# Windowed attention before a feed-forward layer: the attention recast in blocks of 32 queries over 128 keys each

## The chip, the cores and the metric

One core of a Trainium2 chip runs the kernel. The metric is the device time of one execution in microseconds (us), the median over runs.

## What is computed

Eight batches, eight heads, 512 local and 32 global positions, head size 64. A local query sees the 32 global keys and the local keys at most 32 positions away; a global query sees all 544 keys. The attention output (rows of 8 x 64 = 512 values, 544 rows a batch) goes through a feed-forward layer (FFN) with 2048 hidden values.

```python
s_ll = np.where(np.abs(pos[:, None] - pos[None, :]) <= 32, scale * q_l @ k_l.T, -1e9)
a_l = sm(np.concatenate([scale * q_l @ k_g.T, s_ll], axis=-1))
out_l = a_l @ np.concatenate([v_g, v_l])
out_g = sm(scale * q_g @ k_all.T) @ v_all
h = x @ w_in
out = (h - np.tanh(h)) @ w_out
```

Everything is float32, the FFN weights come in as float64.

## The kernel before, in words

Every FFN operand is held as two tiles, the value rounded to TensorE's one-pass float32r format (`hi`) and the remainder (`lo`); a product is three one-pass matmuls, hi*hi, hi*lo and lo*hi. A chunk of the FFN is one batch's 512 local rows: 16 steps, each with 12 matmuls of 512 columns at L1520 (`add_hidden`), tanh on ScalarE, a subtraction on VectorE, the split into `g hi` and `g lo` (L1537 is the low part), and 12 matmuls of 512 columns at L1568 (`add_out`). A last, smaller chunk does the 256 global rows.

Attention goes by pairs of heads, 32 pairs in all, four to a batch. The two heads lie on partitions 0 to 63 and 64 to 127. A pair goes in four tiles of 128 queries. A tile's scores are taken over 224 keys (192 around the tile and the 32 global ones), L1149 in `scores`. For batches 2 to 7 the keys and queries are split into hi and lo (`add_split`) and each score tile is three one-pass matmuls; for batches 0 and 1 they are full float32 matmuls. The mask is added and the row's extreme taken on VectorE (L1458), the exponential on ScalarE (L1465), the reciprocal on VectorE (L1221, L1222), the scaling on GpSimd (L1228). TensorE turns the probabilities (L1170 in `transposes`, matmuls with the identity), two copies bring them to `keys_first`, and `add_product` multiplies them with the values (L1247), four key ranges for each half of the queries. `PARTS` lists the ranges; the values lie in six overlapping ranges of 96 local rows and the 32 global ones. The scores of the global queries are at L1339 (L1079 and L1080 in the first two batches), their probabilities are turned on VectorE (L1381, L1384), in the first two batches on TensorE (L1117).

The order of the work is made when the program is built. Class `Order` holds every operation with an engine (or several to choose from), an estimated duration, a due time and what it reads and writes; `run` lists them by a simulated clock. Eight PSUM banks are dealt out: banks 0 to 3 to attention and to the FFN's hidden step, banks 4 to 7 to the FFN's output. `add_visit` glues several attention operations together so that TensorE does them one right after the other; such a visit asks for all its banks at once. In `add_both` a visit is a pair's transposes of one half followed by scores of another half, which takes four banks. `fill` (L1814) puts matmuls of no use into TensorE's early gaps. Batch 0's attention comes first, with nothing beside it but the loading and splitting of weights; from then on, batch b's attention is woven into batch b-1's FFN chunk.

The first loads of a pair's keys and queries come row by row and TensorE turns them (L1046); from batch 2 on they come in blocks that VectorE turns (L1285).

Of the kernel before, what the change touches and what calls it, by code (L numbers as in the profile page):

```python
# [18 lines left out]
KC = 224  # L19
KG = 352  # L20
# [29 lines left out]
class Order:  # L50
# [14 lines left out]
    def add(self, eng, fn, due, r=(), w=(), res=(), alloc=(), free=(), lat=0.0, xfer=0.0, rows=1.0, ldw=0.107, tail=0.107, lock=False, mode="f", glue=None):  # L65
# [12 lines left out]
        for k in tuple(w) + tuple(res):  # L78
            for x in self.readers.get(k, ()):
                before[id(x)] = x  # L80
        for x in before.values():
            x.succ[id(o)] = o
            o.n += 1
# [121 lines left out]
def kernel(ctx, tc, q_l, k_l, v_l, q_g, k_g, v_g, w_in, w_out, out):  # L205
# [14 lines left out]
    NPG = 736  # L220
    pg = cp.tile([P, NPG], F32, name="pg")
    idr = cp.tile([P, P], F32R, name="idr")
    idn = f32(idr)
    first_kw2 = cp.tile([P, 2 * KG], F32, name="first_kw2", tag="kw")
    first_g = cp.tile([P, H // 2, G], F32, name="first_g", tag="kgt")
# [3 lines left out]
    raw1, kq = rawkq[:, :S], rawkq[:, S:]  # L229
# [4 lines left out]
    gq = cp.tile([P, H // 2, 2, 2, G], F32R, name="gq")  # L234


    prob2 = [t.rearrange("p (a c) -> p a c", a=2)[:, j] for t in tt_ for j in range(2)]

# [12 lines left out]
    first_raw = [first_raw[:, 0], first_raw[:, 1], rawkq.rearrange("p (a t h d) -> p a t h d", a=2, t=NT, h=2)]  # L251
    first_kw = cp.tile([P, 2, 2 * S], F32, name="first_kw", tag="x_lo1")
    first_kw = [first_kw[:, 0, :2 * KG], first_kw[:, 1, :2 * KG], first_kw2]
    first_q = cp.tile([P, 4 * DM], F32, name="first_q", tag="w_out_lo4")
    wide = [wpair, first_q[:, 2 * DM:].rearrange("p (n k) -> p n k", k=2), stage[:, 0], stage[:, 1]]
    first_q = [first_q[:, :S], first_q[:, S:2 * S], cp.tile([P, S], F32, name="first_q2", tag="hi0")]
    first_q = [x.rearrange("p (t c) -> p t c", t=NT) for x in first_q]
    keys_first = cp.tile([P, 2, 2, 2, 384], F32, name="keys_first", tag="kf")
    values = cp.tile([P, 2, 6, D], F32, name="values")

    SETS = [[f"{n}{u}" for n in ("rk", "rq", "pw", "pk", "pq")] for u in range(2)] + [["raw", "kq", "kw0", "kg0", "hk0"]]


    kw_parts = Later(cp, [P, 2 * KG], "kw"), Later(cp, [P, 2 * KG], "hl")
    q_parts = Later(cp, [P, S], "hi0"), Later(cp, [P, S], "wraw2")
    gk = Later(cp, [P, 2, H // 2, G], "kgt")
# [5 lines left out]
    masks = [cp.tile([P, KC], BF16, name=f"mask{j}") for j in range(NT)]  # L272
    stats = [cp.tile([P, 24], F32, name=f"st{j}") for j in range(2)]
    gt = cp.tile([P, 6, G], F32, name="gt")
    prob = [cp.tile([P, 2 * KC + G], F32, name=f"prob{j}") for j in range(2)]
    prob = [prob[t // 2][:, t % 2 * KC:t % 2 * KC + 256] for t in range(NT)]
    first_m = cp.tile([P, 2 * KG], F32, name="first_m", tag="hl")
# [607 lines left out]
    def base(i):  # L885
        if i < H:
            return i * P0
# [963 lines left out]
```

## Time and profile before

| | us |
|---|---|
| median of 3 runs | 975.21 (974.84 to 975.99) |
| span of the profiled execution, first to last instruction | 973.7 |
| TensorE (PE) busy in it | 960.3 |
| VectorE (DVE) busy | 580.3 |
| ScalarE (ACT) busy | 452.1 |
| GpSimd (POOL) busy | 387.3 |

The profile is one execution, and of its own time the page gives the span alone; the median of the runs is 1.5 us above it, 0.15%. Busy times of PE count a matmul from its start to its modelled end, and neighbours overlap, so the spacing of starts is the better measure of what a matmul costs. An x and a number behind a group is its count of instructions. A float32 matmul call stands in the trace as two instructions (L1247 has 16 calls a pair and 32 instructions), a float32r one as one.

### The profile page before, as it was taken

What the parts mean: (1) busy time and instruction counts of PE and PEld (TensorE: products, weight loads), DVE (VectorE), ACT (ScalarE), POOL (GpSimd) and SP (SyncE); (2) the same over time, 40 slices, a digit from 0 to 9 for tenths busy, and PEclk for the clock granted to TensorE, in tenths of its full rate; (3) what the DMA queues carried; (4) which work ended last, traced back from release to release, by engine and by line L of the source; (5) the groups of instructions that cost most, each with busy time, mean ns of one, the idle gap of its engine ahead of it and who ended that gap; (6) DMA issues with size and microseconds to landing.
All of it is one profiled execution on the core that took longest, in us unless ns stands there. A gap on an engine that the chain in (4) does not pass through costs nothing.

```text
span 973.7 us, 18494 instructions
## 1 busy us (share of the span) xinstructions
PE 960.3 (99%) x6453; PEld 784.5 (81%) x6453; DVE 580.3 (60%) x1907; ACT 452.1 (46%) x1275; POOL 387.3 (40%) x526
## 2 busy tenths in 40 slices
PE   8899999999999999999999999999999999999998
PEld 5677877888888888888888888888888888888897
DVE  6997667766657555766676567657636544422211
ACT  6966575745455434654355444534535434111111
POOL 4666756534444433434234444333332332211221
PEclk9999999999999999999999999999999999999999
DMA  8565244321223121322123122221202200100010
GB/s 233 151 178 165 84 114 114 92 38 35 50 39 82 33 39 34 88 40 34 32 38 83 23 39 39 71 50 34 50 14 69 39 17 1 44 1 1 1 44 22
DMA packets 195166, 57.32 MB, mean 59 GB/s; under 512 B 179712, under 2 KB 188416, under 8 KB 195072
## 3 DMA queue, kind: packets, MB, share of 16 engines
q1 hardware_dynamic: 193728, 55.61, 24.1%
q8 instruction: 51, 0.84, 0.4%
q10 hardware_dynamic: 1344, 0.52, 0.2%
q14 instruction: 43, 0.35, 0.1%
HBM read 47.19 MB, written 8.91 MB: 58 GB/s over the span
## 4 chain that ended last, share of the span: by engine, by line
PE 93%; DVE 2%; ACT 2%; SPq 1%; issue 1%; DMA 1%; POOL 0%; POOLq 0%; DVEq 0%; ACTq 0%
PE bank L1520 39%; PE bank L1568 38%; PE bank L1247 6%; PE bank L1149 4%; PE bank L1170 4%; PE bank L1339 1%; SPq L1030 0%; PE bank L1046 0%; DMA wraw<-in_q_g_dram 0%; ACT t L1465 0%; ACT pg L1090 0%; POOL prob L1228 0%; DVE keys_first L869 0%; ACT prob L1465 0%; ACT keys_first L869 0%
## 5 line engine op out<-in xcount | busy, mean ns | idle before, releaser
L1537 POOL TENSOR_TENSOR glo<-t,ghi 128x512 fp32r<-128x512 f32 x107 | 139.1, 1301 | 328.9 <-PE bank L1568 130.0
L1528 ACT ACTIVATE t<-bank 128x512 f32<-128x512 f32 x136 | 81.3, 598 | 302.7 <-PE bank L1520 292.3
L1531 DVE TENSOR_TENSOR t<-bank,t 128x512 f32<-128x512 f32 x136 | 93.9, 691 | 202.5 <-ACT t L1528 201.8
L1228 POOL TENSOR_SCALAR prob<-prob,st 128x224 f32<-128x224 f32 x240 | 108.0, 468 | 143.3 <-DVE st L1222 124.9
L1568 PE MATMUL bank<-w_out_hi,ghi 128*128 128x512 f32 x544 | 152.7, 394 | 0.0
L1568 PE MATMUL bank<-w_out_hi,glo 128*128 128x512 f32 x544 | 151.5, 392 | 0.0
L1568 PE MATMUL bank<-w_out_lo,ghi 128*128 128x512 f32 x544 | 151.3, 392 | 0.0
L1520 PE MATMUL bank<-x_hi,w_in_hi 128*128 128x512 f32 x512 | 140.3, 397 | 0.3 <-DVE x_hi L869 0.3
L1520 PE MATMUL bank<-x_lo,w_in_hi 128*128 128x512 f32 x512 | 137.4, 390 | 0.0
L1520 PE MATMUL bank<-x_hi,w_in_lo 128*128 128x512 f32 x512 | 136.2, 390 | 0.0
L1465 ACT ACTIVATE prob<-prob,st 128x224 f32<-128x224 f32 x240 | 113.2, 475 | 14.9 <-DVE st L1458 13.7
L1458 DVE CUSTOM_DVE_ANT_0 prob<-bank,mask 128x224 f32<-128x224 f32 x240 | 80.8, 386 | 64.7 <-PE bank L1149 57.8
L1568 PEld LDWEIGHTS bank<-w_out_lo,ghi 128*128 128x128 f32 x544 | 101.1, 188 | 22.1 <-issue 1.0
L1568 PEld LDWEIGHTS bank<-w_out_hi,glo 128*128 128x128 f32 x544 | 101.0, 188 | 21.9 <-issue 0.7
L1568 PEld LDWEIGHTS bank<-w_out_hi,ghi 128*128 128x128 f32 x544 | 100.2, 188 | 22.2 <-issue 1.4
L1520 PEld LDWEIGHTS bank<-x_hi,w_in_hi 128*128 128x128 f32 x512 | 93.7, 188 | 24.7 <-issue 3.2
L1520 PEld LDWEIGHTS bank<-x_lo,w_in_hi 128*128 128x128 f32 x512 | 95.9, 188 | 20.2
L1520 PEld LDWEIGHTS bank<-x_hi,w_in_lo 128*128 128x128 f32 x512 | 95.7, 188 | 19.7
L869 ACT COPY keys_first<-bank 128x512 f32<-128x512 f32 (+2 forms) x150 | 69.9, 516 | 89.2 <-PE bank L1170 88.3
L1247 PE MATMUL bank<-keys_first,values 128*64 128x160 f32 (+3 forms) x1024 | 68.7, 276 | 2.2 <-DVE keys_first L869 1.1
L1247 PEld LDWEIGHTS bank<-keys_first,values 96*64 96x64 f32 (+1 forms) x1024 | 56.3, 136 | 9.5 <-ACT keys_first L869 2.9
L1381 DVE STREAM_TRANSPOSE gt<-pg 32x128 f32<-32x128 f32 x192 | 53.1, 276 | 10.2 <-POOL pg L1360 4.3
(164 smaller groups left out, 1222.9 us busy)
## 6 DMA issues: line engine op xcount, KB each, us to landing
values<-in_v_l_dram SPq DMA_DIRECT2D x128, 72.0 KB, 2.2
out_dram<-wpair SPq DMA_DIRECT2D x32, 256.0 KB, 2.0
rawkq<-in_k_l_dram SPq DMA_DIRECT2D x96, 64.0 KB, 2.3
rawkq<-in_q_l_dram SPq DMA_DIRECT2D x96, 64.0 KB, 2.2
values<-in_v_g_dram SPq DMA_DIRECT2D x64, 48.0 KB, 2.0
first_q<-in_moe_w_in_dram SPq DMA_DIRECT2D x6, 512.0 KB, 4.5
stage<-in_moe_w_out_dram SPq DMA_DIRECT2D x6, 512.0 KB, 4.0
stage<-in_moe_w_in_dram SPq DMA_DIRECT2D x6, 512.0 KB, 4.0
```

The lines of the kernel that those rows point to most:

```text
L869: (nc.scalar.copy if e == "A" else nc.vector.tensor_copy)(dst, src)
L1149: nc.tensor.matmul(x[:, i, :KC], q, k, start=n == 0, stop=n == len(passes) - 1)
L1228: nc.gpsimd.tensor_scalar(x, x, st[:, c:c + 1], 1.0, op0=ALU.mult, op1=ALU.mult)
L1247: nc.tensor.matmul(box["o"][h.e:h.e + D, o0:o0 + c1 - c0], values[:k, h.two, t + t // 2 + a], keys_first[:k, h.two, pair, a, c0:c1], start ...
L1381: nc.vector.transpose(gt[r, :c], view(src, [(P, c), (1, 32)], 32 * q))
L1458: nc.vector.tensor_tensor_reduce(out=self.pt(2 * tp + i)[:, :KC], in0=getattr(self, f"s_{tp}")[:, i, :KC], in1=masks[2 * tp + i], scale=-0 ...
L1465: nc.scalar.activation(x, x, AF.Exp, bias=col[:, c0 + i:c0 + i + 1], scale=-1.0, accum_out=col[:, 8 + tp + c0 + i:9 + tp + c0 + i])
L1520: nc.tensor.matmul(self.h[s][:, j * n:(j + 1) * n], w[:, cc, f * P:(f + 1) * P], self.x()[xi][:, cc, :n], start=part == 0 and cc == 0 and ...
L1528: nc.scalar.activation(tt_[q], self.h[s], AF.Tanh)
L1531: nc.vector.tensor_sub(tt_[q], self.h.pop(s), tt_[q])
L1537: eng[e].tensor_sub(gg[q][1], tt_[q], f32(gg[q][0]))
L1568: nc.tensor.matmul(self.acc[tt], g[:, j * self.n + tt * P:j * self.n + (tt + 1) * P], low_out(f) if wi else high_out(f), start=s == 0 and ...
```

## The change

Queries go in 16 blocks of 32. Each block has its own 96 local keys (`window(b)`: its own block and the two beside it) and the 32 global keys: 128 keys in place of 224. Scores are float32 for all batches and keys and queries are no longer split; TensorE is addressed as tiles of 64 rows by 32 columns (`tile_position`), one tile for each head and each of a group's four blocks. Four blocks make 128 rows by 128 keys, so a pair's probabilities are 128 x 512 for each head and are turned with 16 transposes in place of 32. The values lie in 14 ranges of 96 local rows and the 32 global ones, one for each window, so that a product has a block's window as its stationary side. Global queries' scores are float32 too, on tiles of 64 x 32, with the keys cut in two rows of 288 that have to exchange their extreme and their sum (`swap`); their probabilities are turned on VectorE for all batches. Batch 1 is loaded as the later batches are. A pair's TensorE work comes in two visits: scores and global scores, and the last pair's products with this pair's transposes. The due times, nudges and choices of engines of the order are new, and glued operations are ordered by a dependency.

The core of the diff (tables of due times left out):

```diff
-    def keys_of(x, t):
-        c = t // 2 * KG + t % 2 * P
-        return x[:, c:c + KC]
+    def window(b):
+        return min(max(b, 1), NB - 2) - 1
...
-                for i in range(2):
-                    for n, (qi, ki) in enumerate(passes):
-                        for a, x in zip(self.heads, t_):
...
-                            nc.tensor.matmul(x[:, i, :KC], q, k, start=n == 0, stop=n == len(passes) - 1)
...
+        def scores(self):
...
+                t_ = self.box["s"] = [bank([P, S], tags[n]) for n in names]
+                for t in range(NT):
+                    for i in range(4):
+                        b = 4 * t + i
+                        for c, o, n in ((W * window(b), 0, 3 * W), (S, 3 * W, G)):
+                            for h, x in enumerate(t_):
+                                r = slice(64 * h, 64 * h + 64)
+                                nc.tensor.matmul(x[W * i:W * i + W, t * P + o:t * P + o + n], q[r, W * b:W * b + W], kw[r, c:c + n],
+                                                 start=True, stop=True, tile_position=(64 * h, W * i), skip_group_check=True)
...
+        def global_scores(self):
...
+                for i in range(3):
+                    for h, x in enumerate(t_):
+                        r, o = slice(64 * h, 64 * h + 64), 64 * h
+                        c = 3 * W * (2 - i)
+                        nc.tensor.matmul(x[o:o + W, 3 * W * i:3 * W * i + 3 * W], q[r, 1, self.jj], kw[r, c:c + 3 * W],
+                                         start=True, stop=True, tile_position=(o, o), skip_group_check=True)
+                        if i == 0:
+                            nc.tensor.matmul(x[o + W:o + 2 * W], q[r, 1, self.jj], kw[r, 8 * W:], start=True, stop=True,
+                                             tile_position=(o, o + W), skip_group_check=True)
...
+            def swap(c):
+                for i in range(4):
+                    nc.vector.tensor_copy(s[W * i:W * i + W, c + 1:c + 2], s[W * (i ^ 1):W * (i ^ 1) + W, c:c + 1])
...
-                    for i in range(2):
-                        src = a.pt(2 * tp + i)
-                        for c in range(2):
-                            m, c0 = 96 if c != i and self.j >= 6 else P, (96 if i else P) * c
-                            for x in range(2):
-                                r = slice(64 * x, 64 * x + 64)
-                                nc.tensor.transpose(box[x][:m, h, 2 * c + i], src[r, c0:c0 + m], idn[r, r])
...
+                for h in range(2):
+                    for t in range(NT):
+                        for x in range(2):
+                            r = slice(64 * x, 64 * x + 64)
+                            nc.tensor.transpose(box[x][:, h, t], self.prob[h][r, t * P:t * P + P], idn[r, r])
...
+                src, at = pg[64 * h:64 * h + 64, self.u], kf[:, h]
+                for q in range(3):
+                    r = slice(W * q, W * q + W)
+                    nc.vector.transpose(view(at[r], [(G, 3), (1, G)]), view(src[:W], [(3 * W, 3), (1, W)], W * q))
+                    nc.vector.transpose(view(at[r], [(G, 2), (1, G)], S + 4 * G), view(src[W:], [(3 * W, 2), (1, W)], W * q + W))
+                nc.vector.transpose(at[64:96, S + 3 * G:S + 4 * G], src[W:, 7 * W:8 * W])
+                nc.vector.transpose(at[96:, 2 * G:3 * G], src[W:, 8 * W:])
...
-            def keys_low(e, _):
-                for dst, high, src in zip(windows(kw_parts[1]()), windows(f32(kw_parts[0]())), rows(kq)):
-                    eng[e].tensor_sub(dst, src, high)
...
+            def keys(e, _):
+                nc.vector.transpose(kws[2][:, :S], raw[0])
...
-    PARTS = [[(0, 0, P, (0, 160), 0), (1, 0, 96, (64, 160), 64), (0, 1, 96, (192, 288), 160), (1, 1, P, (160, 320), P)],
-             [(0, 2, P, (0, 160), 0), (1, 2, 96, (32, 160), 32), (0, 3, 96, (192, 256), 160), (1, 3, P, (160, 320), P)]]
...
+                parts = [(8, L + 256, 0, 1, 0), (9, L + 288, W, 1, 0), (10, L + 320, 64, 2, E + G - L - 320), (11, L + 352, 96, 1, 0),
+                         (12, L + 384, 128, 1, 0), (13, L + 416, 160, 2, E + 2 * G - L - 416), (14, L + 448, 192, 3, W)]
...
+                parts = [(1, 2 * G, 0, 3, W), (2, L + 64, G + 64, 1, 0), (3, L + 96, G + 96, 1, 0), (4, G, 0, 2, L + 128 - G),
+                         (5, L + 160, G + 160, 1, 0), (6, L + 192, G + 192, 1, 0), (7, 0, 0, 2, L + 224)]
...
+                        nc.tensor.matmul(dst, values[:, h, window(b)], src, start=n == 0, stop=n == len(parts) - 1, skip_group_check=True)
...
+                    nc.sync.dma_start(values[:96, h], bass.AP(v.tensor, v.offset, [[D, 96], [W * D, NB - 2], [1, D]]))
+                    nc.sync.dma_start(values[96:, h], bass.AP(g.tensor, g.offset, [[D, G], [0, NB - 2], [1, D]]))
...
+        p.add_visit(p.at, [p.scores(), p.global_scores()])
+        p.add_softmaxes()
+        p.add_global_softmax()
+        p.add_visit(p.at + 9.0, (last.products() if last.b else []) + [p.transposes()])
```

## Rows read from the trace of the kernel before

**Rows 1.** The page, busy time of the engines; granted clock in 40 slices.

```profile
PE 960.3 (99%) x6453; PEld 784.5 (81%) x6453; DVE 580.3 (60%) x1907; ACT 452.1 (46%) x1275; POOL 387.3 (40%) x526
...
PEclk9999999999999999999999999999999999999999
```

**Rows 2.** The page, the chain that ended last, shares by engine.

```profile
PE 93%; DVE 2%; ACT 2%; SPq 1%; issue 1%; DMA 1%; POOL 0%; POOLq 0%; DVEq 0%; ACTq 0%
```

**Rows 3.** Timeline of PE, around the first FFN matmul: start, us, work.

```profile
58.53 0.71 PE L1520 MATMUL bank<-x_hi,w_in_hi 128*128 128x512 f32 x2
```

**Rows 4.** Windows, all engines: stretch, length, PE, PEld, DVE, ACT, POOL busy (count), PEclk, DMA, GB/s.

```profile
20.00:60.00 40.00, 35.44 (x404) 26.88 (x403) 37.90 (x134) 34.51 (x116) 26.47 (x37) 1.00 0.57 153
```

**Rows 5.** Timeline of PE, two FFN groups in a row.

```profile
521.02 1.07 PE L1520 MATMUL bank<-x_hi,w_in_hi 128*128 128x512 f32 x4
521.93 1.07 PE L1520 MATMUL bank<-x_hi,w_in_lo 128*128 128x512 f32 x4
```

**Rows 6.** Windows, line L1520 on PE (FFN hidden): stretch, length, busy (count).

```profile
58.50:200.00 141.50, 59.74 (x240) 1.00 0.45 121
200.00:800.00 600.00, 252.80 (x1048) 1.00 0.21 44
```

**Rows 7.** Windows, line L1568 on PE (FFN output).

```profile
58.50:200.00 141.50, 54.51 (x212) 1.00 0.45 121
200.00:800.00 600.00, 255.90 (x1044) 1.00 0.21 44
```

**Rows 8.** Windows, line L1247 on PE (products of attention, 32 instructions a pair).

```profile
58.50:200.00 141.50, 11.74 (x151) 1.00 0.45 121
200.00:800.00 600.00, 45.71 (x717) 1.00 0.21 44
```

**Rows 9.** Timeline of PE, a visit with transposes and scores.

```profile
516.75 0.39 PE L1568 MATMUL bank<-w_out_hi,glo 128*128 128x512 f32 x1
517.07 0.69 PE L1170 MATMUL bank<-idr,prob 64*128 64x64 f32 x16
517.57 0.35 PE L1149 MATMUL bank<-kw,hi 64*128 64x224 f32 x2
...
518.40 0.50 PE L1568 MATMUL bank<-w_out_hi,ghi 128*128 128x512 f32 x1
518.74 0.40 PE L1568 MATMUL bank<-w_out_lo,ghi 128*128 128x512 f32 x1
```

**Rows 10.** Timeline of PE, both products of a pair.

```profile
537.52 2.05 PE L1247 MATMUL bank<-keys_first,values 128*64 128x160 f32 x32
539.50 1.20 PE L1520 MATMUL bank<-x_hi,w_in_hi 128*128 128x512 f32 x4
540.53 1.07 PE L1520 MATMUL bank<-x_lo,w_in_hi 128*128 128x512 f32 x4
```

**Rows 11.** Timeline of PE, the global scores of a pair.

```profile
527.37 0.43 PE L1339 MATMUL bank<-kw,gq 128*128 128x256 f32 x2
...
527.89 1.08 PE L1568 MATMUL bank<-w_out_hi,ghi 128*128 128x512 f32 x4
```

**Rows 12.** Timeline of PE, one half's product: its first two, three and all instructions.

```profile
35.80 0.36 PE L1247 MATMUL bank<-keys_first,values 128*64 128x160 f32 x2 [0.28 <-DVE keys_first L869]
...
35.80 0.49 PE L1247 MATMUL bank<-keys_first,values 128*64 128x160 f32 x3 [0.28 <-DVE keys_first L869]
...
35.80 1.10 PE L1247 MATMUL bank<-keys_first,values 128*64 128x160 f32 x16 [0.28 <-DVE keys_first L869]
36.83 0.27 PE L1117 MATMUL bank<-idr,pg 64*128 64x64 f32 x1
```

**Rows 13.** Groups of DVE by line and form: busy, mean ns of one, idle before.

```profile
L1458 DVE CUSTOM_DVE_ANT_0 prob<-bank,mask 128x224 f32<-128x224 f32 x240 | 80.8, 386 | 64.7 <-PE bank L1149 57.8 <-POOL glo L1537 6.6
L1381 DVE STREAM_TRANSPOSE gt<-pg 32x128 f32<-32x128 f32 x144 | 43.2, 300 | 9.4 <-POOL pg L1360 4.3 <-ACT keys_first L869 3.0
...
L1357 DVE RECIPROCAL st<-st 64x1 f32<-64x1 f32 x24 | 3.7, 155 | 0.8
```

More of the change, by code (lines that the diff above doesn't have):

```diff
@@ L80, in add @@
                 before[id(x)] = x
+        if glue is not None:
+            before[id(glue)] = glue
         for x in before.values():
@@ L1272, in add_split, with load @@
+            add(either(512, "qs", True), queries, due + 0.5, r=[qt], w=[pq], free=[(qt, 1)])
         def add_split(self):
-            def load(src):
+            def load(a, src):
                 def fn(e, _):
@@ new lines, in fn, with queries @@
+                            nc.sync.dma_start(raw[a][p0:p0 + 32].rearrange("s (b d) -> s b d", d=32), x[:, :, 32 * half:32 * half + 32])
+                return fn
+            def keys(e, _):
+                nc.vector.transpose(kws[2][:, :S], raw[0])
+            def queries(e, _):
+                nc.vector.transpose(qs[2], raw[1])
+            for a, src in ((0, k_l), (1, q_l)):
+                add(("S", 2.2), load(a, src), self.at - 14.0, w=[self.key[a]], xfer=1.46)
+            add(("D", 0.69), keys, self.at - 3.0, r=["raw0"], w=["kw0"])
@@ new lines, in add_visit @@
+        def add_visit(self, due, parts):
+            own = [n for x in parts for n in x["names"]]
+            reads = [k for x in parts[1:] for k in x["r"] if k not in parts[0]["r"]]
+            after = [k for x in parts[1:] for k in x["res"]]
+            last = None
+            for i, x in enumerate(parts):
+                last = add(("T", x["d"]), x["fn"], due, r=x["r"] + (reads if i == 0 else []), w=x["names"], res=x["res"] + (after if i == 0 else []),
+                           alloc=[(n, self.tag) for n in own] if i == 0 else (), rows=x["rows"], ldw=x["ldw"], tail=x["tail"],
+                           mode=x["mode"], glue=last)
@@ new lines, in first_attention, with attention @@
+        p.add_softmaxes()
+        p.add_global_softmax()
+        for h in range(2):
+            p.add_global_transpose(h)
+        p.add_visit(p.at + 8.0, [p.transposes()])
+        p.add_turned()
+        p.add_visit(p.at + 10.0, p.products())
+        p.add_outputs()
+    def attention(j):
+        p, last = pairs[j], pairs[j - 1]
+        if p.jj == 0:
+            add_globals(p.b)
+        p.add_split()
+        p.add_common()
+        p.add_visit(p.at, [p.scores(), p.global_scores()])
+        p.add_softmaxes()
+        p.add_global_softmax()
+        p.add_visit(p.at + 9.0, (last.products() if last.b else []) + [p.transposes()])
+        if last.b:
+            last.add_outputs()
+        p.add_turned()
+        p.add_values()
+        for h in range(2):
+            p.add_global_transpose(h)
@@ L1776 @@
         ffn_steps(chunk, NF, NF + 1)
+    pairs[-1].add_visit(pair_at(len(pairs)) + 6.0, pairs[-1].products())
+    pairs[-1].add_outputs()
     ng = B * G
@@ L1798 @@
             split_xg(cc)
-        last = Chunk(xgs, [("xg", cc) for cc in range(NCC)], ng, "g", global_rows, chunk.due - (60 if CFG["gfirst"] else -400))
-        chunks = [last, chunk] if CFG["gfirst"] else [chunk, last]
+        last = Chunk(xgs, [("xg", cc) for cc in range(NCC)], ng, "g", global_rows, chunk.due + 104.0)
+        chunks = [chunk, last]
     else:
@@ L1807 @@
         order.ops[i].due += x
+    for i, x in HOLD.items():
+        order.ops[i].ready = x
     for i, x in CHOICE.items():
```

725 lines of the change are left out of this document (237 added, 488 removed), and 627 rows, old and new, of tables (CHOICE, NUDGE).

## The prediction

> **What bounds the kernel now.** I read the page first: PE is busy 99% of a span of 973.7 us, VectorE 60%, and the granted clock is full (2.4 GHz) in all 40 slices [rows 1]. Busy is not the same as bound, so next the chain that ended last: 93% of it is PE, no other engine has more than 2% [rows 2]. So outside the start PE's instructions are the time, one after the other, and what a change is worth is how much shorter it makes PE's stream.
>
> The start is different. The first FFN matmul begins at 58.5 us [rows 3], and from 20 to 60 us VectorE is busy 37.9 of 40 us and ScalarE 34.5 [rows 4]: until batch 0's attention is done the FFN cannot begin, and there VectorE is the fullest engine.
>
> Then I priced PE's stream. FFN matmuls come in groups of four, 0.91 us apart [rows 5], 0.227 us each. From 200 to 800 us there are 1048 + 1044 of them [rows 6, 7], 475 us; the other 125 us are attention, and 717 instructions of the products at 32 a pair are 22.4 pairs [rows 8]: **5.6 us a pair**. From 58.5 to 200 us, 240 + 212 FFN matmuls take 103 us and 39 are left for 4.7 pairs: 0.7 of the later kind (3.9 us) and the four of batch 1 at **8.8 us**. These already hold all waits. They should be compared with pieces: a visit with transposes and scores takes 1.53 us (from 516.98, where the FFN matmul before it has had its 0.227, to 518.40, and 0.11 more because the first FFN matmul after it lasts 0.34) [rows 9], of which the 16 transposes are 0.50, the scores 0.83, the changes in and out 0.20. Two of these, both products at 1.98 and 0.12 of entry [rows 10] and global scores at 0.52 [rows 11] make 5.7, near the mean of 5.6. So PE has nothing to give but these pieces.
>
> **The change, part by part.**
>
> *Scores.* 24 matmuls a pair (three passes, four tiles, two heads), 2 x 0.83 us, become 64 float32 calls, 128 instructions. What decides is how many of the eight tiles of 64 x 32 work at once. The nearest row is one half's product: each head has 160 + 128 + 64 + 160 = 512 columns in float32, on its own half of the array's columns, and both heads together take 35.80 to 36.83, 1.03 us, or 2.0 ns a column of one tile [rows 12]. The first two instructions, 0.35 us each, end 0.36 us after the start, so they start within 0.01 us; the first three end at 0.49, so the third starts at least 0.14 later. In program order the second belongs to the same head as the first; the one that started beside the first must be the other head's, ahead of it. Tiles that share the rows but not the columns therefore run side by side, and an instruction that waits for its own tile does not hold up another. Each of the eight tiles gets 4 x (96 + 32) = 512 columns: 1.03 us if all run side by side. Half of its 16 instructions have 32 columns only; a transposes' step (16 instructions, two row halves at once, 8 steps in 0.50) is 62 ns where 32 columns would be 32, which would add 8 x 0.03: 1.27. I take **1.1**, bounds 1.0 and 1.27.
>
> *Global scores.* 288 columns a tile at 2.0 ns: **0.58** for 0.52, at most 0.75. *Transposes.* 16 for 32: **0.50** for 1.0. *Products.* 704 columns a head in place of 1024. At the 1.98 us for 1024 that is 1.36; 16 steps of 32 columns could each cost 0.03 more: 1.84. I take **1.6**. *Changes of kind.* Two visits of two kinds each for two visits, products and global scores: by the 0.20 and 0.12 above **0.7**, bounds 0.5 and 0.9.
>
> Sum: 1.1 + 0.58 + 0.5 + 1.6 + 0.7 = **4.5 us a pair**, between 3.9 and 5.3. Batches 2 to 7: 24 x (4.5 - 5.6) = -26.4. Batch 1, which now goes the same way: 4 x (4.5 - 8.8) = -17.2. The bounds are -17 and +22 over 28 pairs.
>
> *VectorE and the start.* A peak over 128 columns in place of 224 costs between 221 and 386 ns, about 300: 8 x 0.09 less a pair. For batch 0 the global probabilities are now turned on VectorE, 16 transposes a pair at up to 0.30, and the exchange of extreme and sum adds some 10 tiny instructions at about 0.15 [rows 13]: up to 6 us more a pair, 24 over batch 0, on the engine that is fullest there. Against it: only two turned copies a pair and not four, a smaller global copy, and by 58.5 us VectorE has done a good part of the weights and of batch 1's first pair, which can wait. I take **0**, bounds -6 (PE and ScalarE have less to do) and +15. In batch 0's chunk, where weights still come in, I add **2** for waits on VectorE, bounds 0 and 6. Later the splitting of keys and queries goes away (VectorE, ScalarE and GpSimd) and VectorE stays near 60%: nothing.
>
> *DMA.* The values are 14 ranges and not 6, in rows of 256 bytes, 0.9 MB a pair for 0.4. The DMA engines are at 0.57 from 20 to 60 us [rows 4]; the load has a pair's time, over 10 us, to land. SP issues 4 value loads a pair for 6. I cost it at nothing; if a product had to wait for it, it would show in the start, within the +15. *New waits.* The second visit needs the last pair's turned probabilities and values, due a pair's time before, and this pair's scaling on GpSimd, which is less busy than now; FFN matmuls stand behind it on PE and would wait if it came too soon. The order lists it 9 us after the scores, the span of several FFN groups: nothing. *Banks.* A visit asks for four banks at once, as `add_both` does now, and there are fewer of them: nothing.
>
> Sum: -26.4 - 17.2 + 0 + 2 = -41.6 on a span of 973.7: 932.1. The median of the runs is 1.5 above the span: **933.5**.
>
> **The rivals.**
>
> *Order holds the tiles back (slower).* A block's four instructions lie on one tile in a row: 96, 96, 32, 32 columns. If a waiting instruction holds all that follow it on its half of the rows, only the last runs beside the next block's first. At 1.0 ns a column for one instruction (two make the 2.0) that is 0.096 + 0.096 + 0.032, or 0.22 us a block, 3.6 us for 16 blocks. A pair is then 7.0 us: 24 x 1.4 - 4 x 1.8 + 2 = +28.4, **1003.5**. It decides from 2.6 us of scores on, where the 41.6 is spent. For it: no row shows more than two column tiles, or an instruction that overtakes more than its tile's one other. Against it: rows 12. The Trainium skill, TensorE: Matmul & The Clock Gate, section Part 3, The mechanism, says that matmuls start and end strictly in program order; the same rows disagree with that for two tiles.
>
> *Every start has its price (slower).* If the 31 ns of one transposing instruction (0.50 us for 16) [rows 9] were paid for each of 128 instructions, however they are tiled, scores would be 4.0 us, a pair 7.4, and the sum 24 x 1.8 - 4 x 1.4 + 2 = +39.6: **1015**. Against it: two starts within 0.01 us. The Trainium skill, TensorEngine Tiling (Array Packing), section Instruction Overhead, speaks for it: about 60 cycles of overhead for each matmul whatever its columns, and the advice not to take the tiling from a dimension that is already small. At 2.4 GHz that page's figure is 25 ns, an estimate of 3.2 us for the scores. The trace disagrees across tiles, and cannot tell for 32 columns on one tile.
>
> *Half of the tiles at once.* The overtaking reaches only one block ahead: 2.1 us of scores, +1.0 x 28: **961.5**. Rows 12 fit this as well as my forecast.
>
> *VectorE becomes the bound of the start.* The +15 above, with PE's gain as forecast: **948.5**. For it: 37.9 of 40 busy. Against: the weights can wait.
>
> **How the numbers follow.** Forecast 0.58, VectorE at the start 0.18, half of the tiles 0.13, order 0.08, a price for every start 0.03. The forecast's own range, 915 to 955, is made by the bounds above; with VectorE's case and half of the tiles the range is 912 to 960. Faster by over 0.2% (2 us, about what a measurement can tell) 0.88: the first three; slower 0.10 and same 0.02 from the last two (the order's case, softened, passes through zero).
>
> **What would show it.** Right: FFN groups still 0.91 apart; a scores visit of about 1.1 us for 128 instructions, with eight tiles' starts close together; 16 transposes in 0.5; products near 1.6; first FFN matmul near 58 us; attention from 200 to 800 us near 4.5 us a pair. Wrong: scores of 2 us or more; the first FFN matmul beyond 65 us with VectorE full until then; PE idle between visits waiting for banks.

## The result: slower by one per cent

The changed kernel takes 984.9 us (984.3 to 987.9), the kernel before 975.5 us beside it: a ratio of 1.010, 95% interval 1.0085 to 1.0116. The forecast was 933.5 us, and slower had a chance of 0.10. The profiled execution has a span of 982.2 us, 8.5 more than that of before.

The page of the changed kernel: the busy line [rows 1], the granted clock in 40 slices, PE's instruction queue, and the chain by engine [rows 2].

```profile
PE 947.7 (96%) x10434; PEld 775.0 (79%) x10434; DVE 485.9 (49%) x2066; ACT 403.2 (41%) x1117; POOL 337.2 (34%) x510
...
PEclk9989999999999999999999999999999999999999
...
q8 instruction: 82, 1.34, 0.6%
...
PE 85%; DVE 5%; DMA 3%; issue 2%; ACT 2%; SPq 1%; POOL 1%; POOLq 0%; DVEq 0%; ACTq 0%
```

PE is no longer the whole chain: 15% of it are others. PE has 62% more records, and the clock, full throughout before, is reduced in some early slices. The time by stage, from the first hidden matmul of one chunk to that of the next (us):

| stage | before | after | forecast change | change |
|---|---|---|---|---|
| first FFN matmul | 58.5 | 65.8 | 0 | +7.3 |
| first period (batch 0's chunk) | 118.4 | 127.9 | -15.2 | +9.5 |
| six later periods | 656.4 | 648.2 | -26.4 | -8.2 |
| last chunk, to the last matmul | 136.2 | 135.9 | 0 | -0.3 |

Three things are to be read in the trace. **The FFN groups** are further apart. PE's timeline of batch 3's chunk, an odd one, in the changed kernel:

```profile
505.92 1.09 PE L890 MATMUL bank<-x_lo,w_in_hi 128*128 128x512 f32 x4
506.84 1.08 PE L890 MATMUL bank<-x_hi,w_in_lo 128*128 128x512 f32 x4
507.76 1.09 PE L938 MATMUL bank<-w_out_lo,ghi 128*128 128x512 f32 x4
```

They are 0.92 us apart, not 0.91 [rows 5]. The mean from start to start after 200 us, over spacings under 0.3 us, is 229.9 ns for 227.4. It does so in the last chunk too, with no attention beside it: there the matmuls of x_hi with w_in_hi keep 227 ns and those of x_lo take 231.

**The attention** is cheaper, though not by as much as forecast. Scores with global scores, then a visit with products and transposes (PE's timeline):

```profile
501.74 1.66 PE L639 MATMUL bank<-kw,q 64*32 64x96 f32 x118
...
503.97 1.20 PE L938 MATMUL bank<-w_out_hi,ghi 128*128 128x512 f32 x4
...
514.29 1.95 PE L803 MATMUL bank<-kf,values 128*64 128x96 f32 x56
516.18 0.72 PE L763 MATMUL bank<-idr,prob 64*128 64x64 f32 x16
516.82 0.73 PE L938 MATMUL bank<-w_out_hi,glo 128*128 128x512 f32 x2
```

Products 1.89, transposes 0.64, scores and global scores 2.23 with their exit. The 128 starts of a scores visit cover 1.61 us, the last ones mixed with the global scores. Summed from each start on PE to the next over five periods (20 pairs), attention is 4.63 us a pair; the same sum before is 5.33.

**The start and the first period** have waits that were not there before. Windows of the changed kernel (columns as in [rows 4]), then PE's waits in the start and in the first period (who waited for whom: us in all, times, longest):

```profile
20.00:60.00 40.00, 29.71 (x746) 25.08 (x746) 34.84 (x185) 23.07 (x87) 13.56 (x33) 0.92 0.81 193
66.00:194.00 128.00, 115.81 (x1399) 90.34 (x1398) 102.34 (x371) 76.94 (x210) 75.42 (x92) 0.99 0.64 162
```

```profile
PE bank L639 <- issue: 3.5, 3, 1.7
PE bank L589 <- DMA first_raw<-in_k_l_dram: 3.3, 2, 2.6
PE bank L655 <- issue: 2.3, 2, 1.9
...
PE bank L890 <- DVE st L670: 3.9, 1, 3.9
PE bank L938 <- ACT ghi L408: 2.4, 3, 1.7
PE bank L890 <- ACT w_in_hi L408: 2.1, 2, 1.8
PE bank L890 <- DVE x_lo L836: 1.1, 1, 1.1
```

In the same period before, PE was busy 117.6 of 118.5 us. DMA is busier in both windows (0.81 for 0.57 in the first), VectorE only a little less full in the first (34.8 of 40).

### The profile page after: what moved, and what is told of

Its sections match the earlier page's. It is cut to its first block, busy times and chain, and to the rows that moved or that the text cites. A ratio compares the mean times of both kernels' runs of the same rounds, so it can differ in the third digit from the quotient of the medians.

```text
span 982.2 us, 26082 instructions
## 1 busy us (share of the span) xinstructions
PE 947.7 (96%) x10434; PEld 775.0 (79%) x10434; DVE 485.9 (49%) x2066; ACT 403.2 (41%) x1117; POOL 337.2 (34%) x510
## 4 chain that ended last, share of the span: by engine, by line
PE 85%; DVE 5%; DMA 3%; issue 2%; ACT 2%; SPq 1%; POOL 1%; POOLq 0%; DVEq 0%; ACTq 0%
PE bank L938 36%; PE bank L890 36%; PE bank L803 5%; PE bank L639 5%; PE bank L763 2%; PE bank L655 1%; PE bank L658 1%; DMA wpair<-in_moe_w_out_dram 1%; DMA first_raw<-in_k_l_dram 1%; DMA values<-in_v_l_dram 1%; DMA stage<-in_moe_w_in_dram 1%; DMA stage<-in_moe_w_out_dram 1%; DVE st L675 1%; SPq L852 0%; SPq L535 0%
## 5 line engine op out<-in xcount | busy, mean ns | idle before, releaser
L907 POOL TENSOR_TENSOR glo<-t,ghi 128x512 fp32r<-128x512 f32 x136 | 175.2, 1289 | 418.0 <-ACT ghi L408 307.2
L890 PE MATMUL bank<-x_lo,w_in_hi 128*128 128x512 f32 x512 | 140.6, 396 | 1.1 <-DVE x_lo L836 1.1
L890 PE MATMUL bank<-x_hi,w_in_lo 128*128 128x512 f32 x512 | 139.4, 394 | 0.0
L408 ACT CAST ghi<-t 128x512 fp32r<-128x512 f32 x125 | 77.5, 620 | 82.1 <-DVE t L901 81.0
L741 POOL TENSOR_SCALAR prob<-prob,st 128x128 f32<-128x128 f32 x240 | 87.8, 385 | 23.3 <-DVE st L734 15.2
L727 ACT ACTIVATE prob<-prob,st 128x128 f32<-128x128 f32 x240 | 93.2, 390 | 6.0 <-DVE st L719 5.9
L719 DVE CUSTOM_DVE_ANT_0 prob<-bank,masks 128x128 f32<-128x128 f32 x240 | 55.8, 287 | 76.4 <-PE bank L639 72.0
L803 PEld LDWEIGHTS bank<-kf,values 128*64 128x64 f32 x1792 | 59.5, 143 | 13.9 <-issue 8.2
L803 PE MATMUL bank<-kf,values 128*64 128x32 f32 (+2 forms) x1792 | 65.9, 232 | 2.4 <-DMA values<-in_v_g_dram 1.3
L690 POOL TENSOR_SCALAR pg<-pg,st 128x288 f32<-128x288 f32 x32 | 16.2, 507 | 148.4 <-DVE st L733 125.0
```

Source lines behind the costliest of these rows:

```text
L408: (nc.scalar.copy if e == "A" else nc.vector.tensor_copy)(dst, src)
L719: nc.vector.tensor_tensor_reduce(out=self.prob[h][:, c], in0=self.box["s"][h][:, c], in1=masks[:, t], scale=-0.125, scalar=1e30, op0=ALU.a ...
L727: nc.scalar.activation(x, x, AF.Exp, bias=s[:, k:k + 1], scale=-1.0, accum_out=s[:, 8 + k:9 + k])
L741: nc.gpsimd.tensor_scalar(x, x, s[:, k:k + 1], 1.0, op0=ALU.mult, op1=ALU.mult)
L803: nc.tensor.matmul(dst, values[:, h, window(b)], src, start=n == 0, stop=n == len(parts) - 1, skip_group_check=True)
L890: nc.tensor.matmul(self.h[s][:, j * n:(j + 1) * n], w[:, cc, f * P:(f + 1) * P], self.x()[xi][:, cc, :n], start=part == 0 and cc == 0 and ...
```

## The experiments

Each is one edit of the changed kernel unless it says otherwise. The table has the median time in us, the interval of the ratio to the kernel before, and of one profiled execution each the first FFN matmul, the first period and the six later ones (before: 58.5, 118.4, 656.4). Runs whose edit leaves out no work (e1, e3, e4, e14) have starts of 65.9 to 69.3 and first periods of 126.6 to 130.6, so differences within these ranges tell nothing. Later periods that an edit does not touch agree within 0.2 us (648.0 to 648.2).

| run | time | ratio (95%) | start | first | six |
|---|---|---|---|---|---|
| changed kernel | 984.9 | 1.0085-1.0116 | 65.8 | 127.9 | 648.2 |
| e1_aligned | 980.6 | 1.0035-1.0075 | 69.3 | 130.6 | 641.6 |
| e2_values_once | 982.7 | 1.0058-1.0107 | 65.6 | 127.4 | 648.0 |
| e3_tiles_interleaved | 980.3 | 1.0038-1.0068 | 66.7 | 126.9 | 644.6 |
| e4_all_at_zero | 978.0 | 1.0017-1.0038 | 65.9 | 128.2 | 641.7 |
| e5_no_global_turns | 981.7 | 1.0051-1.0087 | 61.1 | 130.4 | 648.1 |
| e6_split_in_three | 1095.8 | 1.1201-1.1267 | 81.5 | 147.5 | 724.5 |
| e7_one_call_of_128 | 968.8 | 0.9922-0.9952 | 64.8 | 127.7 | 634.0 |
| e8_aligned_interleaved | 974.5 | 0.9980-1.0009 | 66.5 | 130.9 | 638.1 |
| e9_weights_light | 984.7 | 1.0089-1.0122 | 66.6 | 127.3 | 648.1 |
| e10_weights_not_loaded | 981.6 | 1.0055-1.0085 | 67.9 | 125.1 | 648.1 |
| e11_before_misaligned | 980.2 | 1.0037-1.0067 | 59.0 | 118.9 | 659.9 |
| e12_one_call_complete | 1021.1 | 1.0454-1.0499 | 80.4 | 152.7 | 645.9 |
| e13_no_turns_at_all | 981.1 | 1.0044-1.0083 | 62.4 | 135.4 | 648.1 |
| e14_tenth_pair_later | 985.8 | 1.0080-1.0128 | 67.6 | 126.6 | 650.6 |
| e15_windows_copied | 966.9 | 0.9896-0.9925 | 66.9 | 129.9 | 628.9 |
| e16_no_late_weights | 974.7 | 0.9989-1.0008 | 65.8 | 117.5 | 648.0 |
| e17_more_fill | 971.6 | 0.9954-0.9979 | 73.7 | 127.8 | 628.9 |

### Where the tiles lie

Before, the weights, the gated tiles and the activations all began at 256 modulo 512 bytes of a partition. In the changed kernel weights, gated tiles and x_hi1 begin at 384, but x_lo1, x_hi0, x_lo0 and the last quarter of w_out's low part at 0: the new kw tile of 2176 bytes shifts what comes after it.

```diff
-    kw_ = cp.tile([P, KW], F32, name="kw")
+    kw_ = cp.tile([P, 640], F32, name="kw")[:, :KW]
```

> The changed kernel with one tile (kw) made 384 bytes longer, so that the activations and the last quarter of w_out (low part) begin at the same place modulo 512 bytes as the other weights and the gated tiles, as all of them did in the kernel before. Theory placement: FFN matmuls go back from a mean of 230.2 ns to 227.5 ns in every chunk, 3168 x 2.7 ns = 8.5 us less, 976.5 us; the start and the first chunk's waits stay. Rival (other traffic on SBUF or the longer instruction stream slows PE's reading): spacing stays at 230 ns and the time at 985 us.

e4 has this line and one more, which puts all of them at 0:

```diff
-    pg = cp.tile([P, 2, 288], F32, name="pg")
+    pg = cp.tile([P, 608], F32, name="pg")[:, :576].rearrange("p (a c) -> p a c", a=2)
```

> As the first of these, with 128 bytes more ahead of all tiles, so that weights, gated tiles and activations all begin at 0 modulo 512 bytes. If what counts is that the tiles agree with one another: 227.5 ns everywhere and 976.5 us as there. If a moving tile that begins at 0 modulo 512 is itself the slow one: all FFN matmuls at 231 to 235 ns, 985 to 995 us.

And the kernel before, with its even chunks' activations moved off by 128 bytes:

```diff
-    values = cp.tile([P, 2, 6, D], F32, name="values")
+    values = cp.tile([P, 800], F32, name="values")[:, :768].rearrange("p (a t d) -> p a t d", a=2, t=6)
```

> The kernel before with one tile (values) made 128 bytes longer, so that the activations of the even chunks begin 128 bytes off the weights modulo 512 (384 against 256), as in the changed kernel, and nothing else moves but masks, extremes and probabilities. Theory placement: FFN matmuls of the even chunks take 229 to 235 ns in place of 227, the odd chunks stay: 4 x 384 x 4.3 ns = 6.6 us more, 981 to 982 us. If placement is not the cause: 975 us.

e1 and e4 are both back at 227.2 ns; e11 went from 227.4 to 228.7. In e1 and e4 the six later periods lose 6.6 and 6.5 us; e1's time came down by less (4.3 us); in its profile the start and the first period are 3.5 and 2.7 us longer. In e11 the time rises by 4.8 us, less than the 6.6 expected. PE's timeline of e4, at the place shown above for the changed kernel:

```profile
506.21 1.07 PE L938 MATMUL bank<-w_out_hi,glo 128*128 128x512 f32 x4
507.11 1.07 PE L890 MATMUL bank<-x_hi,w_in_hi 128*128 128x512 f32 x4
508.02 1.07 PE L890 MATMUL bank<-x_lo,w_in_hi 128*128 128x512 f32 x4
```

So where the two operands of a matmul begin at different places modulo 512 bytes it is slower (227 to some 232 ns), and it is the difference that counts, not the place. The groups right behind such ones are slower too: in the changed kernel's even chunks those of w_out, whose operands agree, take 229 to 232. 128 bytes off was tried, other distances were not.

### What a start on PE costs

```diff
-                    for i in range(4):
-                        b = 4 * t + i
-                        for c, o, n in ((W * window(b), 0, 3 * W), (S, 3 * W, G)):
+                    for loc in (True, False):
+                        for i in range(4):
+                            b = 4 * t + i
+                            c, o, n = (W * window(b), 0, 3 * W) if loc else (S, 3 * W, G)
```

> The changed kernel with the scores' calls in another order: within each 128 columns first the 96-column calls of all eight tiles, then the 32-column calls of all eight, so that eight instructions in a row go to eight tiles in place of two. Theory lookahead (an instruction that waits for its tile holds up those behind it when too many wait): the 128 instructions take 1.1 to 1.2 us in place of 1.48 in the later batches, 32 x 0.3 = 9 us less, 976 us. Rival (each start costs some 11.5 ns whatever its tile, 128 x 11.5 ns = 1.47 us): 1.45 to 1.5 us, 984 to 986 us.

Then the 96 columns cut into three, and 96 + 32 made one (e6 and e7):

```diff
+                        parts = tuple((W * (window(b) + k), W * k, W) for k in range(3)) + parts[1:]
```

> The changed kernel with each 96-column score call cut into three of 32, the same columns in 256 instructions a pair in place of 128. If each start on PE has a price of some 11.5 to 12.6 ns whatever its tile, a scores visit takes 2.9 to 3.2 us in place of 1.61 (first start to last), a steady period (four pairs) is 5 to 6.5 us longer; if columns and waiting for the tile set the time, it stays at 1.6 to 1.8 and the period within 1 us. Theory pages: PE stops at every 256th of its instructions where it has used the last 256 within a few us; each pair of batch 0 now has one page more, so its start gets four more such stops and the first FFN matmul comes 3 to 8 us later (69 to 74 us). All together 1015 to 1045 us by price and pages, 985 to 990 us by columns.

```diff
-                        for c, o, n in ((W * window(b), 0, 3 * W), (S, 3 * W, G)):
+                        for c, o, n in ((W * window(b), 0, P),):
```

> The changed kernel with one score call of 128 columns a block and head (96 of the window and the 32 keys after it, in place of the global keys, so that the global keys' part of the scores is not computed): the same columns in 64 instructions a pair in place of 128. Price for each start: the visit falls to the columns' bound of 1.0 to 1.15 us, a steady period by 1.8 to 2.4 us. Rival (lookahead or columns): 1.5 to 1.6 us, period unchanged. Theory pages: two pages fewer before the first FFN matmul, which comes 2 to 5 us earlier (61 to 64 us). All together 962 to 970 us by price and pages; 983 to 986 us otherwise.

From the first start to the last of a visit: 64 instructions in 0.89 us (e7), 128 interleaved in 1.43 (e3), 256 in 2.71 where nothing stops them (e6): 10.6 to 11.3 ns a start, until the columns are the limit at 0.89. The order as changed costs 1.61, so that the order of the calls (lookahead) is a small part (0.18) and the price for each start the large one. e7's steady periods are 2.6 us shorter (106.8 and 105.9 us in turn for 109.4 and 108.5), 0.65 a pair. PE's timeline of e7, the local scores of a visit, and of e6, where PE stops inside one:

```profile
467.60 1.16 PE L639 MATMUL bank<-kw,q 64*32 64x128 f32 x64
```

```profile
355.55 2.24 PE L642 MATMUL bank<-kw,q 64*32 64x32 f32 x194
359.80 1.21 PE L642 MATMUL bank<-kw,q 64*32 64x32 f32 x56 [2.00 <-issue]
```

The wait "issue" has nobody behind it. Counted through PE's records of matmuls and weight loads, the changed kernel's five such waits in the start (5.8 us) stand at records 705, 961, 1217, 1473 and 1985, 256 or a multiple of it apart, to within one record; e6's first six at 449, 961, 1473, 1729, 2241 and 2497, on the same grid. The instruction queue [page above] moves 82 packets for 20868 such records, one for 254 (before: 51 for 12906, one for 253). In the later periods of the changed kernel there is no such stop: a visit with its 288 records stands between long FFN groups. e6, with 544, has one of about 2 us in most visits: its six later periods are 76 us longer, of which the price for each start explains 24 x 1.1 = 26, and 22 such stops hold 39; the other 11 stay open. That e7 loses most of these stops moved its start by 1.0 us only, for 2 to 5 expected: they are not what its start waits for last.

The Trainium skill, Runtime: NRT & Kernel Launch, section Instruction fetch mechanics, says that instructions come in blocks of 16 KiB, 256 instructions, and calls the cost of crossing a block mostly hidden. The grid of 256 agrees; the cost does not, where PE issues very short matmuls: 0.4 to 1.9 us a stop in the changed kernel's start.

### The start and the first period

```diff
             def load(e, _):
+                if self.b < 2 and self.jj:
+                    return
```

> The changed kernel, but in batches 0 and 1 only the first pair's values are loaded (the other six pairs multiply by those of the first: six loads of 0.92 MB in rows of 256 bytes are left out). Theory DMA: the value loads are what makes keys, queries and weights late in the start and in the first chunk; without them the first FFN matmul comes at 59 to 62 us and not 65.8, and the first chunk's period falls from 127.9 to 119 to 123 us: 972 to 978 us. Rival (PE's own many small instructions and VectorE's order set the start): first FFN matmul 65 to 66, period 127 to 128, 984 to 986 us.

Nothing in the start or the first period moved by more than 0.5 us: the value loads, which DMA's share pointed to, are not the cause. Next VectorE's turns, which do stand in PE's way; VectorE (the turns of batch 2's first pair) and PE in the changed kernel:

```profile
178.92 0.26 DVE L705 STREAM_TRANSPOSE kf<-pg 32x96 f32<-32x96 f32 x1
...
182.50 0.21 DVE L708 STREAM_TRANSPOSE kf<-pg 32x32 f32<-32x32 f32 x1
182.74 0.45 DVE L670 CUSTOM_DVE_ANT_0 pg<-bank,gmask 64x288 f32<-64x288 f32 x1
...
183.84 2.05 PE L890 MATMUL bank<-x_hi,w_in_hi 128*128 128x512 f32 x4 [3.92 <-DVE st L670]
```

```diff
             def turn(e, _):
+                if self.b < 2:
+                    return
                 src, at = pg[64 * h:64 * h + 64, self.u], kf[:, h]
```

> The changed kernel, but in batches 0 and 1 VectorE does not turn the global probabilities (16 instructions, 3.8 us a pair, left out; products use what the tile held). Theory VectorE: these turns are on the chain from 37 to 62 us and hold up the extreme for which PE waits 3.9 us at 180 us, so without them the first FFN matmul comes at 58 to 62 us in place of 65.8 and the first period falls from 127.9 to 121 to 124 us: 973 to 979 us. Rival (the instruction pages and the clock set the start): the first FFN matmul stays at 64 to 66 us, the first period falls by at most 4 us: 981 to 985 us.

> The changed kernel, but VectorE never turns the global probabilities (left out in all batches; the products use zeros there). If the turns are the cause of the first period's waits: the 3.9 us wait for the extreme at 180 us goes, the second chunk begins at 186 to 189 us in place of 193.7 (191.4 where only batches 0 and 1 leave them out), 976 to 979 us. If it is the order: 190 to 192 us, 981 us as without the turns of batches 0 and 1.

The start comes 4.7 and 3.4 us earlier, earlier than in any other run of the changed kernel: there VectorE is a part of the bound. But the first period grows by 2.5 and 7.5 (e13's profile is the slowest of its ten executions), although the wait of 3.9 is 1.3 in e13. In e5 it is 3.9 as before: the turns ahead of it are batch 2's, which e5 leaves in. In e13 PE waits elsewhere, 8.7 us for ghi and 4.8 for w_in_hi, and both medians are only 3 to 4 us lower. Three more moved little: one for the crowd of attention in that period,

```diff
-            self.at = pair_at(j)
+            self.at = pair_at(j) + (22.0 if j == 9 else 0.0)
```

> The changed kernel with the planned time of the tenth pair (the second of batch 2) 22 us later, so that its scores and the ninth's products and the tenth's transposes move from the first chunk's period into the second's. That moves some 5 us of PE's work by itself, which changes no sum. If the crowd of three pairs' attention in 38 us is the cause of the waits: first and second period together, 234.2 us, become 225 to 230 us and the time 976 to 981 us. If not: 233 to 235 us, 984 to 986 us.

(first and second period together 235.2, for 234.2: no gain), and two that make the weights lighter, in pieces 9 to 24 of the 40:

```diff
+        skip = n >= 8 and not half
...
         def low(e, _):
+            if skip:
+                return
...
```

> The changed kernel, but for 16 of the 40 pieces of the weights (from the ninth on, those of 512 columns) VectorE's two steps of the conversion from float64 are left out (the FFN then computes with the rebiased high words). Theory weights: the second chunk begins at 193.7 us because the stream of weights, begun 13 us later than in the kernel before and prepared on VectorE between batch 0's attention, ends at 197 us; the start, the value loads and PE's stream only move the wait. Without the 16 x 1.0 to 1.8 us of VectorE the second chunk begins at 178 to 187 us, and the time falls to 969 to 978 us. Rival (the waits of the first period are attention's own, the turns and the banks): second chunk at 191 to 194 us, 982 to 985 us.

> As the run before it, and the 16 pieces are not loaded nor rebiased on ScalarE either (the FFN computes with what the slots held). If it is VectorE that makes the weights late, this adds little: second chunk within 2 us of the run before it. If it is DMA (the loads wait on SP behind other loads and share the DMA engines with values, keys and queries) or ScalarE: 4 us or more earlier than there.

The second chunk began at 193.9 and 193.0, as before; e9's time is the same, e10's 3.3 us lower. That seemed to clear the weights. But these runs left the last 16 pieces, the halves, as they were, and SP's queue shows what those do. The changed kernel's first, 25th, 26th and last two of the 40 loads of weights; then the first, 25th, 26th and last two in the kernel before:

```profile
22.38 0.50 SPq L465 DMA_DIRECT2D first_q<-in_moe_w_in_dram  x1
...
136.81 0.43 SPq L465 DMA_DIRECT2D wpair<-in_moe_w_out_dram  x1
147.28 0.39 SPq L465 DMA_DIRECT2D wpair<-in_moe_w_in_dram  x1
...
186.77 3.77 SPq L465 DMA_DIRECT2D wpair<-in_moe_w_out_dram  x2
```

```profile
9.71 0.45 SPq L931 DMA_DIRECT2D first_q<-in_moe_w_in_dram  x1
...
108.97 0.35 SPq L931 DMA_DIRECT2D wpair<-in_moe_w_out_dram  x1
120.07 0.37 SPq L931 DMA_DIRECT2D wpair<-in_moe_w_in_dram  x1
...
162.12 5.29 SPq L931 DMA_DIRECT2D wpair<-in_moe_w_out_dram  x2
```

The stream begins 13 us later, and its last loads go out 23 to 28 us later. The late begin alone does not explain that: in e10, where the 16 pieces ahead are not loaded, the load that goes out at 147.28 in the changed kernel comes no earlier. SP waits there 9.8 us for GpSimd's splitting of an earlier piece, which e10 keeps (SP's timeline; then its wait, from 130 to 149 us):

```profile
146.78 0.39 SPq L468 DMA_DIRECT2D wpair<-in_moe_w_in_dram  x1
SPq L468 <- POOL w_out_lo L497: 9.8, 1, 9.8
```

So a run with all pieces from the ninth on left out:

```diff
-        skip = n >= 8 and not half
+        skip = n >= 8
```

> The changed kernel, but from the ninth of the 40 pieces of the weights on nothing is loaded, rebiased or joined (the FFN computes with what the slots held; the copy to the high part and the subtraction stay). If the weights' last pieces set the end of the first chunk, the second chunk begins at 178 to 187 us in place of 193.7 and the time falls to 968 to 978 us. If the waits are those of one engine behind another in orders written for a shorter schedule, others take their place: 190 us or later, 980 us or more.

The first period falls from 127.9 to 117.5 us, and the time by 10.2 to that of the kernel before. e10, which leaves out the first 16 of these 32 pieces, had lost 2.8 and 3.3. **The work on the last pieces of the weights holds up the end of the first chunk.** In the kernel before these loads go out 23 to 28 us earlier, and PE waits 0.9 us in that period. That it is the lateness, and not the mere work in the new order, was not tried, nor which of the loads, ScalarE's step and VectorE's two weighs most. PE's waits in that period of e16:

```profile
PE bank L901 <- DVE st L681: 2.0, 1, 2.0
PE bank L949 <- ACT ghi L409: 1.4, 2, 1.1
...
PE bank L901 <- ACT w_in_hi L409: 0.4, 1, 0.4
```

Of the wait for w_in_hi 0.4 is left; that behind st falls from 3.9 to 2.0 and that for ghi from 2.4 to 1.4, while those for x_lo and glo stay near 1. On VectorE some 3 us of the weights' steps had stood between 173.9 and 179.0 us, ahead of the turns. PE's idle time in the period falls from 12.2 to 6.1 us, 6 of the 10.4. Another 1.5 is the clock: behind the wait of 3.9 us the changed kernel's next two FFN groups take 1.85 and 1.52 us in place of 0.92, at a granted clock of 0.91 from 180 to 200 us; in e16 it is full there. Why the stream begins later was not tried; on SP's queue the 8 loads of batch 1's global keys and queries (13.0 to 18.1 us) and other loads go out ahead of it.

### Complete kernels

e8 joins e4 and e3:

> The kernel of the run with all tiles at 0 modulo 512 bytes, with the scores' calls interleaved over eight tiles as in the third run: two parts that were measured alone, -7 us and -4.6 us against the changed kernel. If they add, 971 to 975 us, which is the time of the kernel before or just under it.

It came out at 974.5, no different from the kernel before. For one call a block, the keys and the 32 global keys must lie side by side. e12 puts the global keys into the keys' tile after every third block, which changes the order of the values' rows:

> A complete kernel from what the runs showed: tiles at one place modulo 512 bytes, and one score call of 128 columns for each block and head. The 32 global keys stand in the keys' tile after every third block of keys, so that any four blocks in a row hold three neighbours and the global keys; masks, the global scores' calls and the rows of the values follow that order. The values take 16 DMAs a pair in place of 4. By the run with one call (968.8 us) and the gain of placement (7 us): 961 to 963 us; up to 6 us more if the added DMA issues on SP make the start later: 961 to 968 us, and faster than the kernel before either way.

It is the worst but one. PE's waits in e12, over the span:

```profile
PE bank L949 <- ACT ghi L408: 17.1, 4, 5.5
PE bank L949 <- ACT wpair L408: 11.4, 8, 2.6
PE bank L809 <- DMA values<-in_v_g_dram: 6.2, 2, 3.6
```

It loses in the start (80.4 us) and the first period (152.7): but for the 11.4 us behind ScalarE's `wpair`, all of PE's longer waits lie there, 12 us for values among them (5.7 more for in_v_l). SP's waits for a free keys' or values' tile are no longer than in the changed kernel (137.9 and 81.1 us for 222.9 and 91.1 over the span). That the 16 value loads a pair in place of 4 are the cause fits, but was not tried by itself. e15 leaves the loads as they are and lets VectorE write each window out:

```diff
-                nc.vector.transpose(kws[2][:, :S], raw[0])
+                nc.vector.transpose(view(kw_, [(P, NB - 2), (1, 3 * W)]), view(raw[0], [(W, NB - 2), (1, 3 * W)]))
...
```

> A complete kernel: all tiles at 0 modulo 512 bytes, and in batches 1 to 7 one score call of 128 columns a block and head. The keys' tile holds each of the 14 windows by itself (its 96 keys and the 32 global keys), which VectorE's transposing of the keys writes with overlap (1344 columns, estimated at 1.9 us in place of 0.7 for 512); DMA issues as in the changed kernel; batch 0 keeps two calls, interleaved over the tiles. By price for each start and placement a steady period is 3.5 to 4.5 us shorter than in the changed kernel and the time 963 to 970 us; if VectorE's 1.2 us a pair more makes PE wait, up to 980 us.

966.9 us, **faster than both**: 0.9% under the kernel before. A steady period is 105.5 us, where the changed kernel has 109.4 and 108.5 in turn.

> The complete kernel with windows copied, with the filling matmuls (which compute nothing that is used) from 3 to 200 us and not 5 to 72, in shorter waits and more in each: 279 in place of 126. If the low granted clock after PE's waits is worth several us and more filling avoids it: the low stretches fall from 28 us in all to under 15, the mean granted clock rises from 0.985 to over 0.99 and the time from 967 to 960 to 964 us. If the waits are not where the planner puts them, or the fill itself holds PE up: 966 to 972 us.

The granted clock rose (0.989 to 0.994 for e15's 0.984 to 0.986), but the start came later (73.7 us), and the time is 4.6 us longer than e15's; which of the added matmuls PE waited for was not looked into.

## Why the prediction was wrong

The span missed its forecast by 50 us: 7 in the start, 25 in the first period, 18 in the six later ones.

*What bounds.* That outside the start PE's instructions are the time held from 200 us on. For the first period it did not.

*Scores* (1.1 between 1.0 and 1.27; measured 1.61). The tiles do run side by side, up to eight, as rows 12 were read. The step that failed here is the bound: the only price given to narrow pieces was 0.03 us each for half of the steps, and no price to a start across tiles. It is 11 ns, and 128 of them are 1.4 us. The rival with a price for every start was right in kind and three times too dear; its row, transposes, has one tile's wait in it. The figure of the Trainium skill cited for it, about 60 cycles by TensorEngine Tiling (Array Packing), section Instruction Overhead, an estimate of 25 ns, is above what these runs show by a factor of two. The rival in which the order holds tiles back gave 3.6 us; what it costs is 0.18. So slower came true by neither of the two rivals that stood for it: the scores' excess is 0.5 us a pair, some 14 of the 50.

*Products* 1.89 for 1.6 (past the upper bound of 1.84), *transposes* 0.64 for 0.50, with entry. By starts a pair is 4.63 us, and 5.33 before. By the prediction's own count, all that FFN matmuls at their mean spacing do not cover, it is 4.9 after, for the forecast of 4.5, and 5.6 before. So the gain is some 0.7 us a pair, not 1.1. Summed by starts over the six later periods, attention is 15.4 us less, in place of 26.4.

*FFN matmuls unchanged* is the other step that failed in the later periods: 6.5 us, by e4, beside the 11 that attention's gain fell short. No rival named the layout of SBUF, and the diff shows the new tile sizes plainly.

*Batch 1, -17.2.* The 8.8 us a pair were a remainder: all of 58.5 to 200 us that FFN records did not cover, over the pairs by products. They held the longer spacing of FFN matmuls beside attention too: from 58.5 to 200 us the 452 take 108.4 us from start to start, not 103. Attention by starts is 28.5 us in the first period of before, some 7 a pair. After, it is 30.1, with five pairs' scores and transposes in the period, but 6 of that are PE's waits: without waits 24.1 for 27.9, or 3.8 less, 6.7 if the fifth pair's visits (2.9) are set aside. In place of 17.2, that is a miss of 10 to 13 us, as large as attention's 11 in all later periods; why a pair of this batch still costs 5.3 us and not 4.6 was not looked into.

*Waits in the first chunk, +2 (0 to 6); "the weights can wait".* This step failed with batch 1's price, and it is what made the first period longer and not only less short: PE waits 12.2 us in it, for 0.9 before. The case of a later start was called unlikely because the weights' work on VectorE could go behind attention. It did go behind, and without the work on the pieces from the ninth on the chunk ends 10.4 us earlier (e16). The range for the wait was put on VectorE alone, while the chain is load, ScalarE, VectorE, GpSimd and the free slot for the next load.

*The start, 0 (-6 to +15).* +7.3 lies within its bounds; VectorE's turns are 3.4 to 4.7 of it (e5, e13), as the rival of the fullest engine had it. PE's stops at the 256th instructions were in no bound.

*DMA at nothing* held for the value loads (e2). *Banks* at nothing did not quite: the 3.9 us at 180 us are PE waiting for a bank behind the turns (1.3 without them, e13).

## What to carry to other kernels

Look at where tiles begin when a change resizes any of them: here operands that disagreed by 128 bytes modulo 512 cost 0.5 to 0.7% of the time, on matmuls nobody touched. Price small matmuls by starts as well as by columns, and make fewer, wider calls even if another engine must copy to allow it (e15). Where a remainder is charged to one part, ask what else is in it; waits in a sum by starts are the same trap. And look for the stream whose last pieces end the stage: an edit that leaves those in place clears nothing.

## What was not expected of the hardware

Two operands' places modulo 512 bytes change a matmul's time, 227 to some 232 ns. Where PE issues very short matmuls it stops for 0.4 to 1.9 us at places that are multiples of 256 instructions apart, and in e6 for some 2 us even in the later periods. The granted clock is full until the end in the kernel before, where PE is busy all along; in the changed kernel it is 0.92 on the mean from 20 to 60 us, a part of them at the lower level of 1.2 GHz, where PE is busy only 29.7 of 40. One kernel's time goes with it roughly: e13's ten executions run from 977.1 us at a mean of 0.995 to 988.0 at 0.988.
